# Seven products in a row, then thirty-six: the order of TensorE's work in the second half of a feed-forward part

## The chip, the core and the metric

One core of a Trainium2 chip runs the kernel. A core has TensorE (PE in the profile: matmuls; PEld are its weight loads), VectorE (DVE), ScalarE (ACT), GpSimd (POOL) and SyncE (SP, which here only issues transfers). Each works through its own list of instructions in order and waits on semaphores for the others. Matmuls write PSUM; VectorE and ScalarE read PSUM and SBUF, GpSimd works on SBUF alone. The metric is the time on the device in microseconds (us), as the median over runs.

## The reference

Attention with a decay, then a feed-forward part on its result. Of the first, what matters here is only that it delivers `x`, 4608 tokens of 512 values. The second is

```python
h = x @ w_in                                   # 512 -> 2048
sp = np.maximum(h, 0.0) + np.log1p(np.exp(-np.abs(h)))
g = h * erf(sp)
return (g @ w_out).astype(np.float32)          # 2048 -> 512
```

## The kernel before

**Tiling.** The 4608 tokens are six pairs of blocks of 384. Half of `w_in` and `w_out` (1024 of the 2048 middle columns) is in SBUF at a time, so that each pair is visited twice: visits 0 to 5 with the first half, 6 to 11 with the second. A visit has four units (`HU` = 4), one for each 256 middle columns; unit n belongs to visit v = n // 4 and has the place k = n % 4 in it. There are 48 units, 0 to 47. The change bears on units 25 to 47.

**Products with w_in.** All values are split into a high and a low part (float32r), and a product is taken as three matmuls, high by high, high by low, low by high. The 2x2 blocks of (256 columns) x (768 tokens) are computed with seven products instead of eight (a Strassen scheme, `PRODUCTS`, line 63). One product (line 186) is six matmuls of 128x384 into PSUM. Two PSUM tiles, m0 and m1, serve a unit, and each is started twice in it: products 0 and 2 go into one, 1 into the other, 3 and 5 into the second again, 4 and 6 into the first. In between, `consume` takes the partial result out: after product 0 ScalarE copies it to `sa` (line 199); after 1 VectorE adds `sa` to it and gets `sb` (202); after 2 ScalarE copies the first `h` (204); after 3 VectorE makes `sc` (207); after 4, 5 and 6 it makes the other three `h` (210). So product i + 2 may start only when the result after product i has been taken out.

**Activation.** For the four `h` tiles of the unit before, ScalarE computes softplus (214), then erf (217), with a table load ahead of each; VectorE multiplies by `h` (`gate`, 220); ScalarE writes the high half `gh` (229) and GpSimd the low half `gl` (230).

**Products with w_out.** `down(n - 2)` (line 249) is 36 matmuls of 128x512 from `gh` and `gl` of the unit before the last, into six PSUM tiles `y`, one for each 128 tokens (tb = 0 to 5), six matmuls for each. They are summed over the four units of a visit. After the visit's last unit, `finish` takes each `y` out: in the first six visits it stores it to a DRAM tile `part_d`; in the last six VectorE adds the stored part, which lies in a tile `yo` (line 279), and SP stores the sum (280). There are four `yo` buffers for six token blocks. `want_part` (260) loads the first four at the start of the unit k = 0 that follows; the loads for tb = 4 and 5 are issued by `finish` right behind the stores of tb = 0 and 1, into the buffers that these stores read, and so wait on SP until the store has landed.

**The next visit's x.** Four tiles `t` are loaded in the unit with k = 1; two sums (`x_sum`, 112 and 114) follow in k = 2, the splits into high (ScalarE, line 122, 128x768) and low parts (`rest_x`, 127, 128x768) and two more sums (131) in k = 3 and the next k = 0. The seven x tiles have one buffer each, so that a tile is overwritten as soon as the product of the unit k = 3 that reads it is done.

**Order.** Nothing is left to a scheduler (`manual_schedule`): each engine runs the instructions in the order in which the program lists them. `step` lists a unit: for each of seven places a product and its `consume`, side work, and a share of the 36 `down` matmuls by the table `YCUT`: six behind each product except the sixth, behind which there are none.

Of the kernel before, what the change touches and what calls it, by code (L numbers as in the profile page):

```python
# [56 lines left out]
NPAIR = NT // PAIR  # L57
NU = FF // (2 * P)
HU = NU // 2
# [10 lines left out]
SOFTPLUS = "softplus"  # L70
# [6 lines left out]
class Moe:  # L77
# [206 lines left out]
    def do(self, *at):  # L284
        for f in self.work.pop(at, []):
            f()

    def step(self, n):

        v, k = divmod(n, HU)  # L290
        up, gates = n < self.n, 1 <= n <= self.n
        downs = self.down(n - 2) if n >= 2 else iter(())
        after = v + 1 < len(self.visits) and n < self.n
        if n >= 2 and (n - 1) % HU == HU - 1 and self.visits[(n - 1) // HU][1]:
            v_ = (n - 1) // HU
            for tb in range(NTB if v_ == len(self.visits) - 1 else 4):
                self.want_part(v_, tb)
        if gates:
            self.softplus(n - 1, 0)
            self.softplus(n - 1, 1)  # L300
        if after and (n == 2 or v and k == 1):
            self.load_x(v + 1)
        for i in range(7):
            if up:
                self.product(n, i)
                self.consume(n, i)
            if up and v and k == 0 and i == 0:
                self.last_x(v, 0)
            if gates and i == 0:
                for q in (2, 3):  # L310
                    self.softplus(n - 1, q)
                for q in range(4):
                    self.erf(n - 1, q)
            if after and i < 2:
                self.next_x(v + 1, k, i)
            if gates and i in (1, 3):
                for q in (i - 1, i):
                    self.gate(n - 1, q)
            if up and v and k == 0 and i in (1, 2):
                self.last_x(v, i)  # L320
            if gates and i == 2:
                self.do(n, "abs")
            if up and i == (2 if gates else 5):
                self.nc.scalar.preload_act_table_set(SOFTPLUS)
            if gates and i in (2, 3):
                for q in (2 * i - 4, 2 * i - 3):
                    self.halve(n - 1, q)
            if after and i >= 2:
                self.next_x(v + 1, k, i)
            for _ in range(YCUT[i + 1] - YCUT[i]):  # L330
                next(downs, None)
            self.do(n, i)
            yield
        for _ in downs:
            pass
        if self.reload:
            self.reload(n)
# [648 lines left out]
```

## Time and profile before

| | |
|---|---|
| median of three runs | 1058.92 us (1057.91 to 1060.29) |
| the profiled execution | 1058.24 us, span of its instructions 1055.9 us |
| granted TensorE clock | 1.000 over the span |
| PE, PEld busy | 1046.7 us (99%), 933.9 us (88%) |
| DVE, ACT, POOL busy | 761.2 (72%), 778.0 (74%), 499.1 us (47%) |
| matmuls with w_in (L186) | 2016 |
| matmuls with w_out (L249) | 1152 with gh, 576 with gl |

The span runs from the first to the last instruction; the profiled execution's time has 2.3 us beside it. A row of the timeline has the start in us from the span's start, the duration of the merged run of equal instructions, the engine, the line, what is written and read, and how many instructions; in brackets, how long the engine had been idle and what ended that. Matmuls overlap, and the end of one is modelled, so the distance between starts tells what one costs. Unit n of 7 to 47 starts 15.64 us behind unit n - 1; unit 25 starts at 675.99 us and unit 47 at 1020.07 us.

### The profile page before, as it was taken

The page shows a single profiled execution, that of the slowest core. Times are in us where ns is not written, and L with a number is a line of the kernel's source. Part 1 is how long each engine was busy: PE and PEld are TensorE (multiplying, and loading weights), DVE is VectorE, ACT ScalarE, POOL GpSimd, SP SyncE. Part 2 cuts the span into 40 slices and gives each one's busy share as a digit, 9 for nine tenths or more (in the row PEclk, how much of TensorE's full clock was granted, in tenths as well). Part 3 has the DMA queues.
Part 4 walks back from the last instruction along what each step waited for, and adds up shares of the span by engine and source line. Part 5 has one row for each costly group of instructions (what it writes and reads, how often), then busy time and mean ns, then how long its engine had stood idle before and what let it go on. Part 6 is the DMA issues. An engine that isn't in the chain of part 4 may idle for free.

```text
span 1055.9 us, 23199 instructions
## 1 busy us (share of the span) xinstructions
PE 1046.7 (99%) x8554; PEld 933.9 (88%) x8554; DVE 761.2 (72%) x1767; ACT 778.0 (74%) x1668; POOL 499.1 (47%) x650
## 2 busy tenths in 40 slices
PE   9999999999999999999999999999999999999998
PEld 7889889888898888999988899899888899999987
DVE  6899999999867887776778755547565565756533
ACT  6988888898867778777778866767675675766662
POOL 3679899987544463453535333223223313313322
PEclk9999999999999999999999999999999999999999
DMA  7587978777513242523505164631303123130121
GB/s 270 198 287 258 325 254 280 243 241 241 189 67 131 71 168 71 210 100 120 180 28 213 60 226 163 229 121 60 120 16 115 51 67 113 61 120 1 50 91 60
DMA packets 70368, 154.91 MB, mean 147 GB/s; under 512 B 6960, under 2 KB 19504, under 8 KB 69232
## 3 DMA queue, kind: packets, MB, share of 16 engines
q1 hardware_dynamic: 70256, 153.43, 41.9%
q8 instruction: 68, 1.11, 0.4%
q14 instruction: 44, 0.36, 0.1%
HBM read 113.41 MB, written 39.99 MB: 145 GB/s over the span
## 4 chain that ended last, share of the span: by engine, by line
PE 90%; DVE 6%; ACT 2%; issue 1%; DMA 0%; POOL 0%; DVEq 0%; ACTq 0%; POOLq 0%
PE y L249 36%; PE m L186 31%; PE s L666 10%; PE o L774 8%; PE xy L737 3%; DVE pr L696 2%; PE s L673 2%; PE z L737 1%; DVE x L127 1%; DVE e L220 1%; ACT L217 0%; ACT e L217 0%; PE o L737 0%; DVE pt L746 0%; DVE ta L131 0%
## 5 line engine op out<-in xcount | busy, mean ns | idle before, releaser
L230 POOL TENSOR_TENSOR gl<-e,gh 128x384 fp32r<-128x384 f32 x192 | 223.1, 1192 | 392.4 <-ACT gh L229 392.4
L186 PE MATMUL m<-x,wi 128*128 128x384 f32 x2016 | 396.9, 335 | 1.0 <-DVE h L210 0.9
L186 PEld LDWEIGHTS m<-x,wi 128*128 128x128 f32 x2016 | 357.9, 188 | 28.0 <-DVE h L210 3.1
L249 PE MATMUL y<-wo,gh 128*128 128x512 f32 x1152 | 358.0, 392 | 0.0
L249 PEld LDWEIGHTS y<-wo,gh 128*128 128x128 f32 x1152 | 212.2, 188 | 27.9
L249 PE MATMUL y<-wo,gl 128*128 128x512 f32 x576 | 228.6, 397 | 0.0
L721 POOL TENSOR_SCALAR pr<-pr,st 128x576 f32<-128x576 f32 (+4 forms) x320 | 166.5, 542 | 62.7 <-DVE st L714 32.5
L708 ACT ACTIVATE pr<-pr,st 128x576 f32<-128x576 f32 (+3 forms) x320 | 175.5, 553 | 2.0 <-DVE st L696 2.0
L220 DVE TENSOR_TENSOR e<-e,h 128x384 f32<-128x384 f32 x192 | 142.5, 783 | 21.8 <-ACT e L217 21.8
L696 DVE CUSTOM_DVE_ANT_0 pr<-s,c 128x576 f32<-128x576 f32 (+3 forms) x320 | 136.8, 487 | 14.9 <-PE s L673 13.6
L229 ACT CAST gh<-e 128x384 fp32r<-128x384 f32 x192 | 92.0, 512 | 62.8 <-DVE e L220 61.8
L214 ACT ACTIVATE e<-h 128x384 f32<-128x384 f32 x192 | 94.0, 521 | 59.9 <-DVE h L210 55.6
L666 PE MATMUL s<-k,q 64*128 64x320 f32 (+4 forms) x768 | 128.5, 406 | 1.4 <-DVE st L696 0.7
L249 PEld LDWEIGHTS y<-wo,gl 128*128 128x128 f32 x576 | 107.9, 187 | 22.9
L666 PEld LDWEIGHTS s<-k,q 64*128 64x128 f32 x768 | 91.0, 186 | 27.0 <-issue 12.3
L202 DVE TENSOR_TENSOR sb<-m,sa 128x384 f32<-128x384 f32 x48 | 26.7, 557 | 106.4 <-PE m L186 88.9
L774 PE MATMUL o<-pt,v 128*64 128x128 f32 (+1 forms) x1920 | 102.5, 259 | 0.0
L774 PEld LDWEIGHTS o<-pt,v 128*64 128x64 f32 x1920 | 93.7, 137 | 4.5 <-issue 0.2
L127 DVE TENSOR_TENSOR x<-t,x 128x768 fp32r<-128x768 f32 x77 | 80.8, 1061 | 21.5 <-ACT x L122 21.5
L748 ACT COPY pt<-xy 128x1024 f32<-128x1024 f32 x64 | 64.8, 1012 | 36.9 <-PE xy L737 35.5
L210 DVE TENSOR_TENSOR h<-m,sb 128x384 f32<-128x384 f32 x96 | 53.0, 552 | 50.3 <-PE m L186 50.3
L217 ACT ACTIVATE e<-e 128x384 f32<-128x384 f32 x192 | 84.9, 513 | 0.5
(113 smaller groups left out, 1133.5 us busy)
## 6 DMA issues: line engine op xcount, KB each, us to landing
v<-in_vp_dram SPq DMA_DIRECT2D x32, 576.0 KB, 4.5
c<-cum_d SPq DMA_DIRECT2D x60, 288.0 KB, 5.8
t<-xt_d SPq DMA_DIRECT2D x44, 384.0 KB, 5.4
q<-in_q_dram SPq DMA_DIRECT2D x32, 320.0 KB, 4.9
k<-in_k_dram SPq DMA_DIRECT2D x32, 288.0 KB, 5.4
xt_d<-xo SPq DMA_DIRECT2D x32, 288.0 KB, 2.3
part_d<-yo SPq DMA_DIRECT2D x36, 256.0 KB, 3.1
yo<-part_d SPq DMA_DIRECT2D x34, 256.0 KB, 3.2
```

The lines of the kernel that those rows point to most:

```text
L127: eng.tensor_tensor(out=x[:, 1, kd], in0=self.src[r][:, kd], in1=x[:, 0, kd].bitcast(F32), op=ALU.subtract)
L186: nc.tensor.matmul(out=ps, lhsT=w[:, wp, ws], rhs=x[:, xp, kd], start=first and kd == 0 and j == 0, stop=kd == 1 and j == 2 and i in (1, 2 ...
L214: self.nc.scalar.activation(out=e, in_=self.h[n, q], func=AF.Softplus)
L220: self.nc.vector.tensor_mul(self.e[n, q], self.e[n, q], self.h.pop((n, q)))
L229: nc.scalar.copy(out=gh, in_=e)
L230: nc.gpsimd.tensor_tensor(out=gl, in0=e, in1=gh.bitcast(F32), op=ALU.subtract)
L249: yield nc.tensor.matmul(out=y[tb], lhsT=g[:, cs], rhs=w[:, f, wp], start=first, stop=last)
L666: nc.tensor.matmul(out=s[j][:, at:at + k1 - k0], lhsT=q[HALF[j], PAD + START[i]:PAD + END[i]], rhs=k[HALF[j], k0:k1], start=at in (0, 192, ...
L696: nc.vector.tensor_tensor_reduce(out=to[:, ::-1] if j else to, in0=score, in1=decay_, scale=-0.125, scalar=BIG, op0=ALU.add, op1=ALU.min, ...
L708: nc.scalar.activation(out=seg, in_=seg, func=AF.Exp, bias=st[:, 0, j, m:m + 1], scale=-1.0, accum_out=st[:, 1, j, m:m + 1])
L721: nc.gpsimd.tensor_scalar(out=seg, in0=seg, scalar1=st[:, 2, j, m:m + 1], scalar2=1.0, op0=ALU.mult, op1=ALU.mult)
L774: nc.tensor.matmul(out=o[h, to:to + 64 * (1 + (a < b))], lhsT=v[:, ch, h], rhs=src, start=m == 0, stop=m == len(parts) - 1, skip_group_che ...
```

## The change

Units 25 to 47 are listed by a new function, `long_step`. The seven products with their `consume` come back to back; the 36 `down` matmuls come behind the seventh. The side work has new places: all gates, halves and `finish` are listed behind the seventh product, and so are the sums and splits of x for k = 3 that need it; `rest_x` of x tiles 4 and 6 goes to GpSimd instead of VectorE. Which instructions there are, and on what data, does not change otherwise.

```diff
--- before.py
+++ after.py
@@ -285,8 +285,71 @@
         for f in self.work.pop(at, []):
             f()
 
+    def long_step(self, n):
+
+        v, k = divmod(n, HU)
+        dve, pool = self.nc.vector, self.nc.gpsimd
+        after = v + 1 < len(self.visits)
+        if (n - 1) % HU == HU - 1:
+            for tb in range(4):
+                self.want_part(v - 1, tb)
+        if after and k == 1:
+            self.load_x(v + 1)
+        for i in range(7):
+            self.product(n, i)
+            self.consume(n, i)
+            if k == 0 and i == 0:
+                self.split_x(v, 3)
+                self.rest_x(v, 2, dve)
+            elif k == 0 and i == 1:
+                self.rest_x(v, 3, dve)
+            elif after and k == 2 and i < 2:
+                self.x_sum(v + 1, i, dve)
+            elif after and k == 3 and i == 0:
+                self.split_x(v + 1, 0)
+            elif after and k == 3 and i == 1:
+                self.rest_x(v + 1, 0, dve)
+            elif after and k == 3 and i == 2:
+                self.split_x(v + 1, 1)
+            if i == 2 or i == 0 and k in (1, 2):
+                for q in range(4 if i == 2 else 2):
+                    if (n - 1, q) not in self.e:
+                        self.softplus(n - 1, q)
+        for q in range(4):
+            self.erf(n - 1, q)
+        self.nc.scalar.preload_act_table_set(SOFTPLUS)
+        x = after and k == 3
+        if x:
+            self.late_sum(v + 1, 0, dve)
+            self.rest_x(v + 1, 1, dve)
+            self.split_x(v + 1, 5)
+        for q in (0, 1):
+            self.gate(n - 1, q)
+        for q in (0, 1):
+            self.halve(n - 1, q)
+        if x:
+            self.rest_x(v + 1, 5, dve)
+            self.late_sum(v + 1, 1, dve)
+            self.split_x(v + 1, 4)
+        for q in (2, 3):
+            self.gate(n - 1, q)
+        for q in (2, 3):
+            self.halve(n - 1, q)
+        if x:
+            self.rest_x(v + 1, 4, pool)
+            self.split_x(v + 1, 6)
+            self.rest_x(v + 1, 6, pool)
+            self.split_x(v + 1, 2)
+        for _ in self.down(n - 2):
+            pass
+        self.reload(n)
+        yield
+
     def step(self, n):
 
+        if HU * NPAIR < n < self.n:
+            yield from self.long_step(n)
+            return
         v, k = divmod(n, HU)
         up, gates = n < self.n, 1 <= n <= self.n
         downs = self.down(n - 2) if n >= 2 else iter(())
```

Three places show what moved. The names carry the unit's or visit's number, then the tile's: `m33_1` is product 1 of unit 33, `y7_0` is block tb = 0 of visit 7, `gh31_2` is of unit 31.

**PE, the start of unit 33 (k = 1).** Before:

```order
L186 MATMUL m33_0_11119<-x8_0_10853,wi1_1_9512 128x384 x6
L249 MATMUL y7_0_10702<-wo1_3_10098,gh31_0_11030 128x512 x2
L249 MATMUL y7_0_10702<-wo1_3_10098,gl31_0_11031 128x512
L249 MATMUL y7_0_10702<-wo1_3_10098,gh31_1_11034 128x512 x2
L249 MATMUL y7_0_10702<-wo1_3_10098,gl31_1_11035 128x512
L186 MATMUL m33_1_11142<-x8_5_10907,wi1_1_9512 128x384 x6
L249 MATMUL y7_1_10703<-wo1_3_10098,gh31_0_11030 128x512 x2
L249 MATMUL y7_1_10703<-wo1_3_10098,gl31_0_11031 128x512
L249 MATMUL y7_1_10703<-wo1_3_10098,gh31_1_11034 128x512 x2
L249 MATMUL y7_1_10703<-wo1_3_10098,gl31_1_11035 128x512
L186 MATMUL m33_0_11119<-x8_1_10909,wi1_1_9512 128x384 x6
L249 MATMUL y7_2_10704<-wo1_3_10098,gh31_0_11030 128x512 x2
```

and now:

```order
L186 MATMUL m33_0_11115<-x8_0_10826,wi1_1_9512 128x384 x6
L186 MATMUL m33_1_11128<-x8_5_10897,wi1_1_9512 128x384 x6
L186 MATMUL m33_0_11115<-x8_1_10846,wi1_1_9512 128x384 x6
L186 MATMUL m33_3_11149<-x8_4_10911,wi1_1_9512 128x384 x6
L186 MATMUL m33_4_11158<-x8_6_10924,wi1_1_9512 128x384 x6
L186 MATMUL m33_3_11149<-x8_2_10927,wi1_1_9512 128x384 x6
L186 MATMUL m33_4_11158<-x8_3_10982,wi1_1_9512 128x384 x6
L249 MATMUL y7_0_10775<-wo1_3_10098,gh31_0_11052 128x512 x2
L249 MATMUL y7_0_10775<-wo1_3_10098,gl31_0_11053 128x512
L249 MATMUL y7_0_10775<-wo1_3_10098,gh31_1_11056 128x512 x2
L249 MATMUL y7_0_10775<-wo1_3_10098,gl31_1_11057 128x512
```

The six `y` matmuls that stood between two products stand behind all seven; product 2 (the second `m33_0`) follows product 0 with one product between them.

**DVE, the end of unit 33 and the start of unit 34 (k = 1 and 2).** Here L279 is `finish` of visit 7 and L112 and L114 are `x_sum` of visit 9. Before:

```order
L207 TENSOR_TENSOR sc33_11197<-m33_3_11190,sb33_11149 128x384
L220 TENSOR_TENSOR e32_2_11128<-e32_2_11128,h32_2_11098 128x384
L220 TENSOR_TENSOR e32_3_11130<-e32_3_11130,h32_3_11076 128x384
L279 TENSOR_TENSOR yo7_2_10966<-y7_2_10704,yo7_2_10966 128x512
L210 TENSOR_TENSOR h33_3_11224<-m33_4_11217,sc33_11197 128x384
L279 TENSOR_TENSOR yo7_3_10968<-y7_3_10705,yo7_3_10968 128x512
L210 TENSOR_TENSOR h33_1_11240<-m33_3_11190,sb33_11149 128x384
L210 TENSOR_TENSOR h33_2_11248<-m33_4_11217,sb33_11149 128x384
L279 TENSOR_TENSOR yo7_4_11155<-y7_4_10706,yo7_4_11155 128x512
L279 TENSOR_TENSOR yo7_5_11182<-y7_5_10707,yo7_5_11182 128x512
L112 TENSOR_TENSOR t9_4_11114<-t9_2_11112,t9_3_11113 128x768
L202 TENSOR_TENSOR sb34_11301<-m34_1_11294,sa34_11271 128x384
```

and now:

```order
L220 TENSOR_TENSOR e32_0_11124<-e32_0_11124,h32_0_11001 128x384
L220 TENSOR_TENSOR e32_1_11126<-e32_1_11126,h32_1_11035 128x384
L220 TENSOR_TENSOR e32_2_11145<-e32_2_11145,h32_2_11043 128x384
L220 TENSOR_TENSOR e32_3_11147<-e32_3_11147,h32_3_11027 128x384
L279 TENSOR_TENSOR yo7_0_10965<-y7_0_10775,yo7_0_10965 128x512
L279 TENSOR_TENSOR yo7_1_10967<-y7_1_10776,yo7_1_10967 128x512
L279 TENSOR_TENSOR yo7_2_10969<-y7_2_10777,yo7_2_10969 128x512
L279 TENSOR_TENSOR yo7_3_10971<-y7_3_10778,yo7_3_10971 128x512
L279 TENSOR_TENSOR yo7_4_11216<-y7_4_10779,yo7_4_11216 128x512
L279 TENSOR_TENSOR yo7_5_11226<-y7_5_10780,yo7_5_11226 128x512
L112 TENSOR_TENSOR t9_4_11110<-t9_2_11108,t9_3_11109 128x768
L202 TENSOR_TENSOR sb34_11281<-m34_1_11274,sa34_11267 128x384
```

The six L279 stood among the unit's L207 and L210; they now stand in one run behind the four gates (L220), right ahead of L112 and of unit 34's first `sb`. SP's list has the same order at this place before and now: store of `yo7_0`, load of `yo7_4`, store of `yo7_1`, load of `yo7_5`, then the other four stores.

**POOL, units 31 and 32 (k = 3 and 0).** Before:

```order
L230 TENSOR_TENSOR gl30_0_10873<-e30_0_10817,gh30_0_10872 128x384
L230 TENSOR_TENSOR gl30_1_10877<-e30_1_10819,gh30_1_10876 128x384
L230 TENSOR_TENSOR gl30_2_10900<-e30_2_10830,gh30_2_10899 128x384
L230 TENSOR_TENSOR gl30_3_10904<-e30_3_10832,gh30_3_10903 128x384
L230 TENSOR_TENSOR gl31_0_11031<-e31_0_10970,gh31_0_11030 128x384
```

and now:

```order
L230 TENSOR_TENSOR gl30_0_10902<-e30_0_10848,gh30_0_10901 128x384
L230 TENSOR_TENSOR gl30_1_10906<-e30_1_10850,gh30_1_10905 128x384
L230 TENSOR_TENSOR gl30_2_10916<-e30_2_10852,gh30_2_10915 128x384
L230 TENSOR_TENSOR gl30_3_10920<-e30_3_10854,gh30_3_10919 128x384
L127 TENSOR_TENSOR x8_4_10911<-t8_4_10530,x8_4_10911 128x768
L127 TENSOR_TENSOR x8_6_10924<-t8_2_10528,x8_6_10924 128x768
L230 TENSOR_TENSOR gl31_0_11053<-e31_0_11003,gh31_0_11052 128x384
```

The two L127, which VectorE ran before, stand behind the four `gl` of unit 30 and ahead of those of unit 31; products 3 and 4 of unit 32 read what they write.

## The prediction, on record before the changed kernel ran

> **What bounds the kernel now.** I read the page first, then the sums over units 25 to 47 alone, then TensorE's timeline.
>
> ```profile
> span 1055.9 us, 23199 instructions
> PE 1046.7 (99%) x8554; PEld 933.9 (88%) x8554; DVE 761.2 (72%) x1767; ACT 778.0 (74%) x1668; POOL 499.1 (47%) x650
> 675.99:1035.70 359.71, 359.71 (x1795) 323.32 (x1794) 204.07 (x294) 233.80 (x409) 104.05 (x92) 1.00 0.24 81
> ```
>
> The third row is the stage that the change touches: 359.71 us, PE busy in all of it (the second number), the clock at 1.00. Nothing is waited for there, so TensorE's own pace sets the end, and a gain can only come from that pace. A busy PE is not yet PE at its peak, so I look at the distances between starts. First from product 5 of unit 23 to that of unit 24, then the last 36 matmuls of the kernel, which run without products between them:
>
> ```profile
> 656.87 2.25 PE L186 MATMUL m<-x,wi 128*128 128x384 f32 x12
> 658.96 0.63 PE L249 MATMUL y<-wo,gh 128*128 128x512 f32 x2
> 660.35 1.21 PE L186 MATMUL m<-x,wi 128*128 128x384 f32 x6
> 661.39 0.63 PE L249 MATMUL y<-wo,gh 128*128 128x512 f32 x2
> 662.78 1.20 PE L186 MATMUL m<-x,wi 128*128 128x384 f32 x6
> 672.51 2.25 PE L186 MATMUL m<-x,wi 128*128 128x384 f32 x12
> ...
> 1037.08 0.62 PE L249 MATMUL y<-wo,gh 128*128 128x512 f32 x2
> 1050.68 0.62 PE L249 MATMUL y<-wo,gh 128*128 128x512 f32 x2
> ```
>
> One product takes 661.39 - 660.35 = 1.04, two in a row 658.96 - 656.87 = 2.09: no gain there. A block of six `y` takes 662.78 - 661.39 = 1.39. In the tail 60 `y` lie between the two rows: 13.60 us, 1.36 for six. So each change from products to `y` costs 0.03. A unit is 672.51 - 656.87 = 15.64 now.
>
> **The change, part by part.** *TensorE's pace.* Five of six changes go in each unit. A unit is then 7 x 1.04 + 6 x 1.36 + 0.03 = 15.47, less by 0.17; over 23 units **-3.8 us**. This is all that there is to gain.
>
> *The hand-over of PSUM.* Product i + 2 starts 2.08 behind product i and needs its result taken out.
>
> ```profile
> 1032.40 2.07 PE L186 MATMUL m<-x,wi 128*128 128x384 f32 x11
> 1034.51 0.56 DVE L210 TENSOR_TENSOR h<-m,sb 128x384 f32<-128x384 f32 x1 [0.48 <-PE m L186]
> ...
> 332.10 0.54 DVE L210 TENSOR_TENSOR h<-m,sb 128x384 f32<-128x384 f32 x1
> 332.70 1.31 PE L186 MATMUL m<-x,wi 128*128 128x384 f32 x6 [0.16 <-DVE h L210]
> 333.84 0.63 PE L249 MATMUL y<-wo,gh 128*128 128x512 f32 x2
> ```
>
> A product ends 1.21 behind its start (its row above); VectorE starts 0.04 later (1034.47 to 1034.51), takes 0.56, and a waiting matmul starts 0.06 behind that (332.64 to 332.70): 1.87 of 2.08. The cover that is gone, 1.39 of `y`, is not needed as long as the engine is free within 0.21 us. Cost 0; if every one of the five hand-overs missed by 0.1, it would be 23 x 5 x 0.1 = 11.5. The last two rows also price a restart: that product takes 1.14 instead of 1.04, so 0.1 for each stall.
>
> *The stores and loads behind `finish` (k = 1, felt in k = 2).* Times from here on are from the first product of the unit k = 1. VectorE takes the last `h` out at 7.5 to 8.0, then come four gates, then six L279.
>
> ```profile
> 743.04 1.03 DVE L220 TENSOR_TENSOR e<-e,h 128x384 f32<-128x384 f32 x2 [0.21 <-ACT e L217]
> 743.99 1.28 DVE L279 TENSOR_TENSOR yo<-y,yo 128x512 f32<-128x512 f32 x2
> 744.70 0.35 SPq L280 DMA_DIRECT2D out_dram<-yo  x1
> 746.70 0.33 SPq L260 DMA_DIRECT2D yo<-part_d  x1
> 747.12 0.38 SPq L280 DMA_DIRECT2D out_dram<-yo  x1
> 750.11 0.32 SPq L260 DMA_DIRECT2D yo<-part_d  x1
> ...
> 807.26 0.35 SPq L280 DMA_DIRECT2D out_dram<-yo  x1
> 813.72 0.32 SPq L260 DMA_DIRECT2D yo<-part_d  x1
> ...
> yo<-part_d SPq DMA_DIRECT2D x34, 256.0 KB, 3.2
> ```
>
> Unit 29 began at 738.55 (675.99 + 4 x 15.64), so its first L279 stood at 5.4 and its first store was issued at 6.15; SP holds the load for tb = 4 until that store has landed (2.00), holds the next store behind that load, and the load for tb = 5 until that store has landed: 5.41 from the first store's issue to the last load's, 6.46 in unit 33; then 3.2 to landing (page, part 6). Now the first L279 comes behind the four gates: some 0.5 apart by the row of two, from 8.0, 8.5 and 9.0; the fourth, at 9.5, finds GpSimd's first `gl` begun at 9.4 and waits for it (below), to 10.8. Store at 11.55, last load issued at 17.0, landed at 20.2. The sixth L279 waits for it, and behind it on VectorE stand `x_sum` and unit 34's `sb`, without which product 3 cannot start:
>
> ```profile
> L279 DVE TENSOR_TENSOR yo<-y,yo 128x512 f32<-128x512 f32 x30 | 20.0, 681 | 1.2 <-PE y L249 1.2
> L112 DVE TENSOR_TENSOR t<-t,t 128x768 f32<-128x768 f32 x5 | 4.7, 949 | 0.0
> ```
>
> 20.2 + 0.64 + 0.88 (both a little under their duration, as the next overlaps) + 0.56 + 0.06 = 22.35; product 3 was due at 15.47 + 3.12 = 18.59. Stall 3.75 us in units 30, 34, 38 and 42; in 46 there is no `x_sum`, 2.9. Sum **+17.9**. Low end: gates without the collision (0.8 earlier) and a landing shorter than its median by 0.4 (an estimate), 2.55 each, 11.8 in all; high end: 6.46 in the chain, 4.8 each, 23 in all. I take the middle, since unit 29's row is the shorter of the two and the landing is a median.
>
> *GpSimd's two rests (k = 3, felt in k = 0).* GpSimd and VectorE get in each other's way on SBUF operands:
>
> ```profile
> 778.46 4.58 POOL L230 TENSOR_TENSOR gl<-e,gh 128x384 fp32r<-128x384 f32 x4 [11.20 <-ACT gh L229]
> 778.84 2.34 DVE L220 TENSOR_TENSOR e<-e,h 128x384 f32<-128x384 f32 x2
> 782.50 1.36 DVE L127 TENSOR_TENSOR x<-t,x 128x768 fp32r<-128x768 f32 x1 [0.85 <-ACT x L122]
> L444 POOL TENSOR_TENSOR llo<-ltop,lhi 128x512 fp32r<-128x512 f32 x8 | 10.4, 1299 | 45.7 <-PE m L186 30.3 <-ACT lhi L443 15.4
> L127 POOL TENSOR_TENSOR x<-ta,x 128x384 fp32r<-128x384 f32 x6 | 6.0, 1001 | 0.0
> ```
>
> Two gates took 2.34 beside `gl` against 1.03 above, and four `gl` 4.58 against 4 x 1.0: they run in turns. An L127 that began under a `gl` took 1.36 instead of 0.95. The Trainium skill (SBUF — State Buffer, "SBUF: two separate sides") states that the port pair which the two share is locked for a whole instruction, and the other blocks. By that rule a long instruction on GpSimd holds VectorE off for all of it, and the sum is the one below; were the port given up in between, it would be the low end. The trace agrees for 384 columns (1.36); for 768 on GpSimd no run here shows it yet.
>
> From 384 and 512 columns (1.00 and 1.30) 768 come to about 1.85. ScalarE's list sets the beginning:
>
> ```profile
> 740.16 0.94 ACT L214 ACTIVATE e<-h 128x384 f32<-128x384 f32 x2
> 741.12 1.28 ACT L217 ACT_TABLE_LOAD   x1
> 742.41 1.77 ACT L217 ACTIVATE e<-e 128x384 f32<-128x384 f32 x4
> L122 ACT CAST x<-t 128x768 fp32r<-128x768 f32 x35 | 27.5, 828 | 0.0
> ```
>
> In k = 3: `h` out at 3.3 to 3.8, split of x1 to 4.4, four softplus to 6.1, table to 7.4, erfs to 9.1, table to 10.4, split of x5 to 11.1, `gh` 0 and `gl` 0 from 11.7. On VectorE stand now rest x5, a sum, gates 2 and 3, each in turns with `gl` 0 and 1: gate 3 ends at 15.6, `gl` 2 starts at 15.8, `gl` 3 ends at 17.8. The rest of x4 goes in turn with VectorE's rest of x2 and ends at 20.3, that of x6 with the rest of x3 and ends at 22.9. ScalarE, held by the late `gh`, copies unit k = 0's `sa` at 17.5 to 18.0, 0.8 late, which moves product 2 by 0.5. Product 3 (reads x4) could start at 18.59 + 0.5 and waits until 20.4, 1.2; product 4 (reads x6) then waits from 21.4 to 22.9, 1.4. Stall 3.1 in units 28, 32, 36, 40 and 44: **+15.6**. Low end: no turns, all ends by 19.7, 0.1 each; high end: 2.0 for the rest on GpSimd, 3.45, 17.3 in all. The rows are nearest to the high end, since VectorE's work beside GpSimd's is the same kind.
>
> *Restarts:* 5 x 3 + 5 = 20 stalls at 0.1, **+2.0**. Everything else (other places of gates and halves, `want_part`, `load_x`) has over a unit until it is read: 0.
>
> **Sum:** -3.8 + 17.9 + 15.6 + 2.0 = +31.7 us on the profiled execution's 1058.24, 1089.9. The median of the runs is 0.7 above that execution, so **1090 us**.
>
> **The rivals.**
> - *Only the loads stall, GpSimd is in time* (the low end of that part): 1058.9 - 3.8 + 17.9 + 0.5 = 1073.5. For it: `gl` alone takes 1.0; against it: the 4.58 and 2.34 above. Chance 0.17.
> - *Faster:* if the sixth L279 starts by 18.59 - 0.06 - 0.56 - 0.88 - 0.64 = 16.45, unit 34's `sb` is in time, and if GpSimd also is, what remains is 1058.9 - 3.8 = 1055.1. What decides is whether the last load lands by 16.45; the chain of 5.41 + 3.2 would have to start at 7.8, when the first `y` is not yet summed (7.28 + 1.39). Chance 0.05.
> - *The hand-overs miss* by 0.1 each, beside the stalls: 1090 + 11.5 = 1101.5. For it: only 0.21 of slack; against it: the steps are the same in every row that I looked at. Chance 0.06.
> - *The clock falls behind the long stalls:* if TensorE ran at half speed for the four products behind each stall in k = 2, that is 5 x 4 x 1.04 = 21 more, 1111. Nothing in the trace bears it out; the one idle time over 1 us had no drop of the clock near it:
>
> ```profile
> PE idle L806 <- POOL ident masks.py:199: 1.4, 1, 1.4
> ```
>
> The Trainium skill (TensorE: Matmul & The Clock Gate, "What's actually happening") puts the fall to half at an idle window of about 3.4 us, and 3.75 lies just above it. No run here shows it. Chance 0.07.
>
> **How the numbers follow.** The forecast has 0.65, with its own range 1079 to 1099 from the two terms' ends. Below 1069 lie the faster case and the lower part of the first rival, above 1101 the clock and part of the hand-overs: together 2 in 10. Range 1069 to 1101. About 0.2% is what a measurement can tell from no change; faster by more 0.04, within it 0.02, slower 0.94.
>
> **What would show it.** In the changed profile: `y` rows 0.68 apart for three in all units; units k = 1 and k = 3 at 15.47; PE idle in k = 2 ahead of product 3, ended by VectorE's `sb`, with the sixth L279 idle until a transfer; PE idle in k = 0 ahead of products 3 and 4, ended by GpSimd's L127. It is wrong if units k = 2 or k = 0 take under 16 us, if products without a stall are over 1.05 apart, or if the clock leaves 1.00.

## The result, and the profile after

The changed kernel takes 1090.23 us (median of 6 runs, 1085.29 to 1096.44), the kernel before beside it 1059.51 us (6 runs, 1057.91 to 1060.57). The ratio is 1.0291 with a 95% interval of 1.0255 to 1.0327: slower by 2.9%. The forecast of 1090 is met as a time; its terms are not all met, and misses cancel.

The first lines of the changed kernel's page:

```profile
span 1083.5 us, 23179 instructions
PE 1051.8 (97%) x8554; PEld 936.0 (86%) x8554; DVE 747.2 (69%) x1757; ACT 775.7 (72%) x1668; POOL 521.9 (48%) x660
```

The sum over units 25 to 47 (from and to, us, then busy us and instructions of PE, PEld, DVE, ACT and POOL, granted clock, share of the DMA engines, GB/s):

```profile
675.12:1063.30 388.18, 365.62 (x1795) 325.92 (x1794) 189.61 (x284) 233.26 (x412) 127.27 (x102) 0.99 0.22 75
```

The stage grew from 359.71 to 388.18 us, by 28.5. PE, which was busy in all of it before, is idle for 22.6 us of it (388.18 - 365.62), and the granted clock is no longer 1.00. TensorE's waits in that stage name who ends the idle time (us in total, how often, the longest):

```profile
PE m L186 <- DVE sb L202: 10.0, 5, 2.4
PE m L186 <- POOL x L127: 9.8, 10, 1.2
PE m L186 <- ACT sa L199: 2.8, 5, 0.6
```

That is 20 stalls, where the prediction counted 20: one in each of the five units k = 2 (ahead of product 3, ended by VectorE's `sb`), three in each of the five units k = 0 (the wait ahead of product 2 ended by ScalarE, those ahead of products 3 and 4 by GpSimd). From the distances between the first products of neighbouring units, against 15.64 before:

| units | length now, us | sum against before |
|---|---|---|
| the 12 without a stall, base of all 23 | 15.51 (25 and 26: 15.48 and 15.54) | 23 x -0.13 = -3.0 |
| k = 0: 28, 32, 36, 40, 44 | 18.89, 18.91, 18.88, 18.91, 18.89 | 16.9 over the base |
| k = 2: 30, 34, 38, 42, 46 | 19.82, 17.83, 17.65, 19.75, 17.07 | 14.6 over the base |

The three come to +28.5. Outside the stage the two profiled executions differ by 1.4 the other way, so that this one is 1085.29 - 1058.24 = 27.1 slower; it is the fastest of the six.

**Units k = 0.** The timelines of GpSimd, VectorE and TensorE around the start of unit 32 (791.37; the last row of an engine counts only up to the end of the stretch shown, so that it can be short):

```profile
787.80 3.06 POOL L230 TENSOR_TENSOR gl<-e,gh 128x384 fp32r<-128x384 f32 x2 [13.88 <-ACT gh L229]
791.91 1.98 POOL L230 TENSOR_TENSOR gl<-e,gh 128x384 fp32r<-128x384 f32 x2 [1.04 <-ACT gh L229]
793.85 5.09 POOL L127 TENSOR_TENSOR x<-t,x 128x768 fp32r<-128x768 f32 x2
...
795.14 2.12 DVE L127 TENSOR_TENSOR x<-t,x 128x768 fp32r<-128x768 f32 x1
...
791.37 2.27 PE L186 MATMUL m<-x,wi 128*128 128x384 f32 x12
794.20 1.52 PE L186 MATMUL m<-x,wi 128*128 128x384 f32 x7 [0.55 <-ACT sa L199]
796.50 1.31 PE L186 MATMUL m<-x,wi 128*128 128x384 f32 x6 [0.78 <-POOL x L127]
799.00 2.20 PE L186 MATMUL m<-x,wi 128*128 128x384 f32 x11 [1.18 <-POOL x L127]
```

In unit 31 (which began at 791.37 - 15.51 = 775.86) the first `gl` begins at 11.94, the last ends at 18.0, and the two rests end at 20.6 and 23.1; the prediction had 11.7, 17.8, 20.3 and 22.9. Beside each other the 768-wide subtracts take turns: 5.09 for the two on GpSimd, and 2.12 for one on VectorE that takes 0.95 alone.

**Units k = 2.** SP, GpSimd, VectorE and TensorE around unit 34 (first product at 825.79; unit 33 began at 810.28):

```profile
820.84 0.35 SPq L280 DMA_DIRECT2D out_dram<-yo  x1
822.85 0.33 SPq L260 DMA_DIRECT2D yo<-part_d  x1
823.27 0.38 SPq L280 DMA_DIRECT2D out_dram<-yo  x1
826.22 0.32 SPq L260 DMA_DIRECT2D yo<-part_d  x1
...
819.92 4.09 POOL L230 TENSOR_TENSOR gl<-e,gh 128x384 fp32r<-128x384 f32 x4 [11.59 <-ACT gh L229]
...
818.26 1.95 DVE L220 TENSOR_TENSOR e<-e,h 128x384 f32<-128x384 f32 x4
820.13 1.28 DVE L279 TENSOR_TENSOR yo<-y,yo 128x512 f32<-128x512 f32 x2
829.07 0.69 DVE L279 TENSOR_TENSOR yo<-y,yo 128x512 f32<-128x512 f32 x1 [2.70 <-DMA yo<-part_d]
829.68 0.95 DVE L112 TENSOR_TENSOR t<-t,t 128x768 f32<-128x768 f32 x1
830.55 0.55 DVE L202 TENSOR_TENSOR sb<-m,sa 128x384 f32<-128x384 f32 x1
...
825.79 3.31 PE L186 MATMUL m<-x,wi 128*128 128x384 f32 x18
831.15 1.14 PE L186 MATMUL m<-x,wi 128*128 128x384 f32 x5 [2.05 <-DVE sb L202]
```

Here is the whole chain: a store, a load behind it, a store, a load, the sixth L279 that waited 2.70 for that load, `x_sum`, `sb`, product 3. It is the chain that the prediction named, but it starts earlier than there: the four gates run in 1.95 without a break, and GpSimd's first `gl` begins at 819.92, behind the start of the fourth gate (818.26 + 3 x 0.47 = 819.67).

**The clock.** Units 30 and 42 are 2 us longer than 34 and 38, with idle times that are nearly the same (2.45 and 2.40 against 2.05 and 1.84). The stage in pieces of 3.41 us shows why (same columns as above; the seventh is the granted clock):

```profile
758.69:762.10 3.41, 0.96 (x6) 0.64 (x5) 2.37 (x4) 2.67 (x5) 0.00 (x0) 1.00 0.94 341
762.10:765.51 3.41, 3.41 (x12) 3.41 (x12) 1.07 (x2) 2.97 (x5) 0.00 (x0) 0.51 0.84 296
...
895.20:898.60 3.40, 1.62 (x10) 1.30 (x8) 2.01 (x4) 2.61 (x7) 0.00 (x0) 1.00 0.91 337
898.60:902.00 3.40, 3.33 (x19) 3.33 (x20) 1.99 (x4) 3.37 (x6) 0.00 (x0) 1.00 0.93 316
```

Behind unit 30's stop TensorE has half its clock for one piece (12 matmuls where 19 fit); behind unit 38's it has not.

### The profile page after: what moved, and what is told of

Same layout as the page of the kernel before. It is cut to its first block, busy times and chain, and to the rows that moved or that the text cites. A ratio compares the mean times of both kernels' runs of the same rounds, so it can differ in the third digit from the quotient of the medians.

```text
span 1083.5 us, 23179 instructions
## 1 busy us (share of the span) xinstructions
PE 1051.8 (97%) x8554; PEld 936.0 (86%) x8554; DVE 747.2 (69%) x1757; ACT 775.7 (72%) x1668; POOL 521.9 (48%) x660
## 4 chain that ended last, share of the span: by engine, by line
PE 69%; issue 9%; DVE 8%; POOL 5%; ACT 5%; DMA 3%; SPq 0%; DVEq 0%; POOLq 0%; ACTq 0%
PE y L249 24%; PE m L186 21%; PE s L729 9%; PE o L837 8%; DMA out_dram<-yo 3%; POOL gl L230 3%; PE xy L800 3%; POOL x L127 2%; DVE pr L759 2%; PE s L736 2%; ACT e L217 1%; DVE e L220 1%; PE z L800 1%; ACT L217 1%; ACT e L214 1%
## 5 line engine op out<-in xcount | busy, mean ns | idle before, releaser
L186 PE MATMUL m<-x,wi 128*128 128x384 f32 x2016 | 387.4, 339 | 23.6 <-DVE sb L202 10.0
L220 DVE TENSOR_TENSOR e<-e,h 128x384 f32<-128x384 f32 x192 | 127.8, 714 | 18.4 <-ACT e L217 18.4
L199 ACT COPY sa<-m 128x384 f32<-128x384 f32 x48 | 23.0, 479 | 131.2 <-PE m L186 131.0
L214 ACT ACTIVATE e<-h 128x384 f32<-128x384 f32 x192 | 90.9, 521 | 23.6 <-DVE h L210 18.0
L127 DVE TENSOR_TENSOR x<-t,x 128x768 fp32r<-128x768 f32 x67 | 75.6, 1136 | 26.9 <-ACT x L122 26.9
```

The costliest lines, as they stand in the source:

```text
L127: eng.tensor_tensor(out=x[:, 1, kd], in0=self.src[r][:, kd], in1=x[:, 0, kd].bitcast(F32), op=ALU.subtract)
L186: nc.tensor.matmul(out=ps, lhsT=w[:, wp, ws], rhs=x[:, xp, kd], start=first and kd == 0 and j == 0, stop=kd == 1 and j == 2 and i in (1, 2 ...
L214: self.nc.scalar.activation(out=e, in_=self.h[n, q], func=AF.Softplus)
L220: self.nc.vector.tensor_mul(self.e[n, q], self.e[n, q], self.h.pop((n, q)))
```

## The experiments

The theory after the result: the loss has two independent causes, the chain of stores and loads in k = 2 and GpSimd's rests in k = 0, and on top of the first a fall of the clock behind some of the stops. The rivals: that back-to-back products themselves pay (hand-overs of PSUM, TensorE's pace), that only one of the two causes is real, and that the clock does not fall because of the stop. All edits are against the changed kernel, and each run stands beside runs of the kernel before on its chip.

| run | median, us (lowest to highest) | ratio to before (95%) |
|---|---|---|
| rests on VectorE | 1086.69 (1083.65 to 1089.33) | 1.0258 (1.0230 to 1.0285) |
| own buffers | 1072.24 (1071.96 to 1073.19) | 1.0125 (1.0103 to 1.0147) |
| both | 1067.10 (1066.30 to 1067.84) | 1.0074 (1.0055 to 1.0093) |
| TensorE kept busy | 1084.98 (1083.74 to 1086.23) | 1.0243 (1.0222 to 1.0263) |
| x first, with own buffers | 1056.07 (1054.00 to 1060.00) | 0.9975 (0.9960 to 0.9990) |
| the same, `sc` twice | 1068.25 (1065.85 to 1069.25) | 1.0085 (1.0064 to 1.0107) |
| the change again | 1090.98 (1086.65 to 1093.11) | 1.0295 (1.0270 to 1.0320) |
| both, `gl` later | 1058.24 (1056.62 to 1060.39) | 1.0002 (0.9992 to 1.0011) |

### The two rests back on VectorE

```diff
-            self.rest_x(v + 1, 4, pool)
+            self.rest_x(v + 1, 4, dve)
             self.split_x(v + 1, 6)
-            self.rest_x(v + 1, 6, pool)
+            self.rest_x(v + 1, 6, dve)
```

> The two rests of x4 and x6 go back to VectorE at the place where the change lists them; all else is the changed kernel. Theory (GpSimd, taking turns with VectorE, ends them too late for products 3 and 4 of the unit k = 0): these units go from 18.9 us to about 17.6, since VectorE's queue and the late copy sa still hold product 2 and 3 for 0.7 and 1.4; 5 x 1.3 = 6.5 less, 1084 as a median. Units k = 2 stay at 17.1 to 19.8. Rival (ScalarE is too full in k = 3, and its late copies alone cause the stall): units k = 0 stay at 18.9, 1090.

TensorE's waits in the stage:

```profile
PE m L186 <- DVE sb L202: 16.9, 10, 3.5
PE m L186 <- ACT sa L199: 2.8, 5, 0.6
```

GpSimd ends no wait any more. Units k = 0 take 17.65 instead of 18.9, or 19.22 where the clock fell. The choice of engine is thus 1.25 of the 3.4 us; the other 2.14 stay, now ended by VectorE's `sb` (1.0 of idle time) and ScalarE's `sa` (0.55): the rests still stand behind four `gl` that take turns with VectorE's work. The units k = 2 were longer here, 18.13 to 20.88 (17.24 in unit 46), although nothing was changed for them: the clock fell in three of them instead of two, and the chain was longer in some. So the median fell by some 4 us instead of the 6.5 expected, and the intervals of the two ratios overlap; the length of the units k = 0 is what shows the gain. In unit 34, the longest, SP's rows of the same chain were:

```profile
820.99 0.35 SPq L280 DMA_DIRECT2D out_dram<-yo  x1
823.96 0.33 SPq L260 DMA_DIRECT2D yo<-part_d  x1
824.39 0.38 SPq L280 DMA_DIRECT2D out_dram<-yo  x1
827.62 0.32 SPq L260 DMA_DIRECT2D yo<-part_d  x1
```

It took 6.63 from the first store's issue to the last load's, where the changed kernel's took 5.38: each load could be issued 2.97 and 3.23 behind the store ahead of it, instead of 2.01 and 2.95. The same chain can cost over 1 us more in another execution.

### All six parts of `y` loaded ahead, with buffers of their own

```diff
         if (n - 1) % HU == HU - 1:
-            for tb in range(4):
+            for tb in range(NTB):
                 self.want_part(v - 1, tb)
...
+        elif tb >= 4:
+            yo = self.eb.tile([P, DM], F32, name=f"yo{v}_{tb}", tag="top", bufs=3)
...
-        if tb + 4 < NTB and v + 1 < len(self.visits):
-            self.want_part(v, tb + 4)
```

> In the second half of the visits the stored parts for tb = 4 and 5 get buffers of their own (those of the weight work, which is over by then), and all six are loaded at the start of the unit k = 0; finish issues stores only. Theory (the sixth addition waits for a load that waits for a store, and the next unit's sb stands behind it): units k = 2 go from 17.1 to 19.8 us to 15.5, the clock stays at 1.000 there, units k = 0 stay at 18.9; 1090 - 11 for the stalls - 6 for the clock = 1073. Rival (products in a row outrun the engines that empty PSUM, wherever the side work stands): units k = 2 stay over 16.5, above 1080.

TensorE's waits in the stage:

```profile
PE m L186 <- POOL x L127: 9.8, 10, 1.2
PE m L186 <- ACT sa L199: 2.8, 5, 0.6
```

Two of its units, 30 and 32, whole:

```profile
755.90:771.40 15.50, 15.50 (x79) 14.06 (x78) 7.08 (x12) 8.72 (x16) 4.07 (x4) 1.00 0.39 137
786.91:807.35 20.44, 17.93 (x79) 15.52 (x78) 8.77 (x12) 11.94 (x21) 11.46 (x8) 0.92 0.21 77
```

Every unit k = 2 is now 15.51, and PE is busy throughout (15.50 of 15.50). Taking the store out of the load's way takes 1090.98 - 1072.24 = 18.7 us off (across two chips) with no instruction removed. So the chain of stores and loads was the whole cause there, the clock's falls in these units included. One fall is left, in unit 32, which has the three shorter stops of k = 0 and no long one.

### Both

```diff
-            self.rest_x(v + 1, 4, pool)
+            self.rest_x(v + 1, 4, dve)
...
-            self.want_part(v, tb + 4)
```

> Both of the edits before: the rests of x4 and x6 on VectorE, and own buffers for tb = 4 and 5. Theory: units k = 1, 2, 3 at 15.5, k = 0 at 17.6; 1059.5 - 23 x 0.13 + 5 x 2.1 = 1067. Rival (products in a row outrun the engines that empty PSUM): all units are longer than 15.64 where a consume has company on its engine, and the sum stays over 1075.

TensorE's waits in the stage:

```profile
PE m L186 <- DVE sb L202: 5.0, 5, 1.0
PE m L186 <- ACT sa L199: 2.8, 5, 0.6
```

The units k = 0 take 17.65 (one 19.19 with a fall of the clock), all others 15.51. The two causes add: from the change's 1.0291 the single edits take 0.0033 and 0.0166, together 0.0199, and both at once take 0.0217; the intervals are some 0.002 to 0.004 wide on either side.

### TensorE kept busy in the stop of k = 2

Ten matmuls more, into the first `y` tile of the visit, whose own first matmul comes later in the unit and overwrites them; they stand ahead of product 3 in units 30, 34, 38, 42 and 46. No result changes.

```diff
+            if k == 2 and i == 3 and v > NPAIR:
+                self.keep_busy(v, k)
             self.product(n, i)
...
+        for _ in range(10):
+            self.nc.tensor.matmul(out=y[:, :TB], lhsT=self.wi[1, k][:, 0, 0, :P], rhs=self.x[v, 0][:, 0, 0],
+                                  start=True, stop=True, skip_group_check=True)
```

> The changed kernel with ten more matmuls of 128x384 (1.74 us) in the units 30, 34, 38, 42 and 46, ahead of product 3, where TensorE stands still for 2 us or more; they go into a y tile whose real first matmul starts afresh, so the result is the same. Theory (the clock falls because TensorE stood still for too long): the extra matmuls lie in the stall and cost nothing, the idle time left is under 1 us, the clock stays at 1.000, and the median falls from 1090 to 1081 to 1085, with a smaller spread, though work was added. Rival (the clock and the spread have another cause): the clock still falls in some runs and the median stays at 1090. Second rival (the stall is not there in all runs): the matmuls add up to 5 x 1.74 = 8.7, 1099.

The end of the stop of unit 30 on TensorE's timeline:

```profile
762.09 1.90 PE L293 MATMUL y<-x,wi 128*128 128x384 f32 x10
764.65 1.69 PE L186 MATMUL m<-x,wi 128*128 128x384 f32 x8 [0.67 <-DVE sb L202]
```

Units 30 and 28 whole:

```profile
758.94:777.10 18.16, 17.49 (x89) 15.77 (x88) 8.51 (x13) 8.93 (x16) 4.41 (x4) 1.00 0.37 132
723.10:743.40 20.30, 17.79 (x79) 15.38 (x78) 8.79 (x12) 11.96 (x21) 11.47 (x8) 0.92 0.22 78
```

Product 3 starts when it would have started anyway, but none of the five units k = 2 shows a fall: 18.21, 18.18, 18.27, 18.28 and 17.24. 50 matmuls more make the kernel about 5 us faster (1084.98 against 1090.23 and 1090.98, on other chips; the interval of the ratio lies wholly below that of the change run again and overlaps the lower end of the first one's). So the stop itself costs 18.2 - 15.5 = 2.7 us a unit in this execution, 1.7 in unit 46; what such units take beyond that with a fall was the clock. The one fall left is in a unit k = 0, to which nothing was added.

### The work on x first

All that products of the next unit k = 0 read is listed ahead of gates 2 and 3 in k = 3, on VectorE, and the `gh` and `gl` of the four gates go behind product 0 of the next unit. Own buffers as above.

```diff
+            if k == 0 and v > NPAIR and i == 0:
+                for q in range(4):
+                    self.halve(n - 2, q)
...
+            for q in (0, 1):
+                self.gate(n - 1, q)
+            self.rest_x(v + 1, 5, dve)
+            self.late_sum(v + 1, 1, dve)
+            for r in (4, 6, 2, 3):
+                self.split_x(v + 1, r)
+                self.rest_x(v + 1, r, dve)
+            for q in (2, 3):
+                self.gate(n - 1, q)
```

> The change with both causes taken away: own buffers for tb = 4 and 5 as in the experiment before, and in the unit k = 3 the work on the next x comes first: all splits on ScalarE and all rests on VectorE, gates 0 and 1 in the hole where VectorE waits for the split of x5, gates 2 and 3 last; the four halves (gh and gl) of that unit's gates move behind product 0 of the next unit, so that GpSimd's gl do not start while VectorE works on SBUF tiles. Theory (the stalls come from these two places alone, and the order of products is good by itself): every unit from 25 to 46 at 15.51, TensorE idle nowhere, clock 1.000; 1059 - 23 x 0.13 = 1056, so 0.3% faster than the kernel before. Rival (the order of products costs more than it brings, whatever stands beside it): units over 15.64, and the median over 1059.

The stage as a whole:

```profile
676.68:1033.30 356.62, 356.62 (x1795) 323.41 (x1794) 177.05 (x294) 232.82 (x412) 92.27 (x92) 1.00 0.23 82
```

A unit of it on TensorE's timeline:

```profile
785.24 7.47 PE L186 MATMUL m<-x,wi 128*128 128x384 f32 x42
792.55 0.63 PE L249 MATMUL y<-wo,gh 128*128 128x512 f32 x2
```

PE is busy in all of the stage and the clock is at 1.00: every unit takes 15.51, and 23 of them 356.62 against 359.71 before. Seven products back to back with every hand-over of PSUM in time: 7.31 us for 42 matmuls. This version is faster than both kernels: against the one before by 2.6 us in the median (ratio 0.9975, 0.9960 to 0.9990), of which the stage's 3.1 us, the pace, is the source.

### One addition twice

To measure the slack of the hand-over, VectorE's `sc` is computed twice in units 25 to 47 of the kernel above.

```diff
-            nc.vector.tensor_tensor(out=self.u4, in0=ps, in1=self.u2, op=ALU.add)
+            for _ in range(2 if HU * NPAIR < n < self.n else 1):
+                nc.vector.tensor_tensor(out=self.u4, in0=ps, in1=self.u2, op=ALU.add)
```

> The experiment just before, with the addition that makes sc done twice in units 25 to 47 (same operands, same result), to price the hand-over of PSUM: product 5 waits for it. By the prediction's rows it has 0.21 us to spare (1.87 of 2.08), and the second addition takes 0.48: product 5 is late by 0.27 and restarts for 0.1, so units go from 15.51 to 15.8 to 15.9, and the time by 6 to 9 us to 1062 to 1065. Rival (there is more to spare, as TensorE works ahead): units stay at 15.51, 1056.

TensorE's only wait in the stage:

```profile
PE m L186 <- DVE sc L208: 4.6, 23, 0.2
```

VectorE and TensorE in one unit, from the timeline:

```profile
777.16 1.15 DVE L208 TENSOR_TENSOR sc<-m,sb 128x384 f32<-128x384 f32 x2 [0.60 <-PE m L186]
775.75 2.42 PE L186 MATMUL m<-x,wi 128*128 128x384 f32 x13
778.37 1.83 PE L186 MATMUL m<-x,wi 128*128 128x384 f32 x9 [0.20 <-DVE sc L208]
```

The second addition adds 1.15 - 0.56 = 0.59, more than the 0.47 by which two gates in a row differ from one. Product 5's first matmul stands 13 behind the row's first; it comes 2.62 later (778.37 - 775.75) instead of 13 x 0.174 = 2.26, so 0.36 late. The hand-over therefore takes 2.08 + 0.36 - 0.59 = 1.85 without the doubling, a slack of 0.23; the prediction worked out 1.87 and 0.21. The units are 16.01, 0.50 longer: 0.36 and a restart of 0.14. Both are above what was expected (0.27 and 0.1), and so is the time, 1068.25 against 1062 to 1065: the second addition takes 0.59, where 0.48 had been assumed.

### The change again

No edit; the changed kernel on the chip of the two runs above.

> The changed kernel as it is, once more, beside the others on one chip, for the clock: units k = 2 where TensorE stood still for over 2.3 us have the clock halved for 3.4 us behind it, those with less do not; k = 0 at 18.9 where the clock stays, some 1.5 longer where it falls. Median 1085 to 1092, mean clock of the runs 0.989 to 1.000, and the longer runs are those with the lower clock. Rival (the spread is the transfers', not the clock's): no order between the clock and the time.

Units k = 2 of this execution: 19.88 (30), 19.95 (34), 19.68 (38), 18.18 (42), 17.17 (46); k = 0: 20.31, 20.47 and 20.44, then 18.88 and 18.91. Six units have a fall of the clock, where the first execution had two. Pieces of 3.41 us in units 28 and 42:

```profile
726.06:729.47 3.41, 1.79 (x9) 1.18 (x7) 2.58 (x2) 3.08 (x6) 3.41 (x2) 1.00 0.00 0
729.47:732.88 3.41, 3.07 (x10) 3.07 (x11) 0.56 (x1) 3.38 (x6) 0.29 (x1) 0.50 0.50 150
...
971.82:975.23 3.41, 1.83 (x11) 1.51 (x9) 1.26 (x2) 2.62 (x7) 0.00 (x0) 1.00 0.95 302
975.23:978.64 3.41, 2.59 (x15) 2.60 (x16) 2.38 (x5) 3.38 (x6) 0.00 (x0) 1.00 0.78 210
```

Unit 42 has the same stop as unit 38 (2.40 us idle against 2.33) and no fall: its stop lies across two pieces, for which the rows show 11 and 15 matmuls. Unit 28, whose three stops are 0.55, 0.78 and 1.18, has one. The expectation that the length of one stop decides falls with this; the counts at the end show what goes with a fall instead, how little ran within a piece. The median, 1090.98, lies in the expected range. The longer runs have the lower clock only by and large: 1093.11 at 0.991, 1092.15 at 0.995, 1090.98 at 0.993, 1087.62 at 1.000, 1086.65 at 0.998.

### The rests on VectorE, own buffers, and `gl` later

As "both", with the halves of unit k = 3 listed behind product 0 of the next unit, which leaves the order of x as the change has it.

```diff
-        for q in (0, 1):
+        for q in () if x else (0, 1):
             self.halve(n - 1, q)
...
+                if v > NPAIR:
+                    for q in range(4):
+                        self.halve(n - 2, q)
```

> The kernel with both edits (rests on VectorE, own buffers) and one more: the four halves of the unit k = 3 move behind product 0 of the next unit; the order of the work on x stays. It asks what still holds units k = 0 at 17.65. Theory (GpSimd's gl take turns with VectorE's work on SBUF tiles in k = 3, which makes gates 2 and 3 late, then gh on ScalarE, then sa and sb): the chain is gone, units k = 0 go to about 15.9 (what is left is the copy of the first h, late by 0.4 behind the moved gh), 1067 - 5 x 1.75 = 1058. Rival (VectorE's list in k = 3 is too long by itself, with two more rests): units k = 0 stay at 17.6, 1067.

TensorE's waits in the stage:

```profile
PE m L186 <- ACT h L204: 0.9, 5, 0.2
```

That is the only wait left, and the median is as expected. Against "both", 17.65 of k = 0 become 16.0 by this edit alone. Gates 2 and 3 in unit 31 of "both" (beside `gl`) and of this run:

```profile
784.49 1.83 DVE L220 TENSOR_TENSOR e<-e,h 128x384 f32<-128x384 f32 x2
...
781.83 1.02 DVE L220 TENSOR_TENSOR e<-e,h 128x384 f32<-128x384 f32 x2
```

From the unit's first product they start at 14.06 and 13.22 and end 1.65 apart, as the sum ahead of them took turns with `gl` too (1.78 against 0.95). So the 2.14 which stayed when the rests went back to VectorE go with the four halves' place for the most part, and the rows show GpSimd's `gl` in turns with VectorE's work. The edit takes `gh` off ScalarE's list in k = 3 as well; what that alone brings was not measured apart.

## Why the prediction was right, and where it was wrong

| term | predicted | measured in the profiled execution |
|---|---|---|
| pace of 23 units | -3.8 | -3.0 |
| hand-overs of PSUM | 0 | 0 |
| k = 0, with its restarts | 15.6 + 1.5 | 16.9 |
| k = 2, with its restarts, at full clock | 17.9 + 0.5 | about 11.4 |
| falls of the clock | 0 | about 3.1 |
| sum | 31.7 | 28.4 |

The falls of the clock are two here, taken out of units 30 and 42 at 1.6 each, an estimate by the price that k = 0 shows in the repeated run (20.31, 20.47 and 20.44 against 18.89: 1.4 to 1.6).

**The pace** was right in kind. The one change from products to `y` that is left costs 0.07 rather than 0.03: with it a unit is 15.51, where 42 products and 36 `y` at 7.28 and 8.16 make 15.44. Before, six changes cost 15.64 - 15.44 = 0.20, so the five saved are worth 0.13 a unit.

**The hand-overs** cost nothing, and the slack was right to 0.02, by the run with `sc` twice. This rival (1101.5) is excluded: x first runs all seven back to back with PE never idle.

**k = 0** was right step by step. Products 2, 3 and 4 were put 0.5, 1.2 and 1.4 late; by the starts in unit 32 they are 0.74, 1.09 and 1.45 late (the rows at 796.50 and 799.00 begin with the second matmul of products 3 and 4), 3.28 in all, and the unit is 3.40 longer. The choice of the end near the high one, by the rows in which the two engines take turns, held: a rest on GpSimd took 2.5 in turns, where 1.85 had been worked out for one alone, and all ends lie within 0.3 of those worked out. What the prediction did not say is how the 3.4 splits: the first run above puts 1.25 down to the engine of the rests, the last puts 1.65 down to the halves (`gh` and `gl`) ahead of them. The Trainium skill (SBUF — State Buffer, "SBUF: two separate sides") has it that whichever of the two engines comes first holds the shared port pair for its whole instruction; the rows now agree for 768 columns too, 2.12 against 0.95 on VectorE. The rival "only the loads stall" is excluded by own buffers, where nothing but k = 0 is left and costs 18.9 a unit.

**k = 2** is the step that failed. The mechanism held at each link: removing the store ahead of the load removes every stall of these units. Its size did not. The step is the passage "the fourth, at 9.5, finds GpSimd's first `gl` begun at 9.4 and waits for it (below), to 10.8". GpSimd's first `gl` began at 819.92 - 810.28 = 9.64, behind the fourth gate's start at 9.38, and the four gates ran in 1.95 without a break; the first L279 stood at 820.13 - 810.28 = 9.85. This was no accident of one unit: in all 20 units k = 1 behind unit 28 of the four profiled executions that have this chain, `gl` begins at 9.64 and the fourth gate at 9.38. ScalarE's list, from which the 9.4 for `gl` came, ran some 0.25 later than worked out. The chain of 5.41 was right here (5.38) and the landing shorter than its median (829.07 - 826.22 = 2.85 instead of 3.2). Product 3 came at 20.87 instead of 22.35: 1.0 of the 1.5 is the collision that did not occur, 0.35 the landing, the rest the steps behind. So the low end that the prediction gave, 2.55 each, was near (2.1 to 2.7). A collision that the working decided by 0.1 us should have been counted as open, not as met. The spread of the chain was real as well: 5.38 here, 6.63 in one unit of the run with the rests on VectorE.

**The clock** had a chance of 0.07 and a price of 21. It came, so that the prediction's own last sign of being wrong, a clock that leaves 1.00, is there. It came in another form: not four products behind every stall, but one stretch of 3.41 us at half the clock behind some of them, 1.4 to 1.6 us each, twice in the first profiled execution and six times in the repeated one (two runs whose mean clock is shown as 1.000 had none), and in k = 0 too, where the prediction had not looked for it. The condition that it cited from the Trainium skill (TensorE: Matmul & The Clock Gate, "What's actually happening"), an idle window of about 3.4 us, was not needed: a stop of 2.45 was enough, in a stretch for which the row shows 6 matmuls. The same section of the Trainium skill states that the window runs free of the program. The traces agree: the two falls of the first execution, 762.15 and 966.95, lie 60 x 3.413 us apart, and from unit 25's start the raster stands 1.7 us in there and 2.6 in the repeated execution.

So k = 2 was put some 7 too high, the clock 3 too low in the profiled execution (some 9 in the repeated one), and the pace 0.8 too high a gain. For the profiled execution itself the forecast, 1089.9, was 4.6 too high; it is met by the median only because that lies 4.9 above this execution, where 0.7 had been put. That the time came out to 0.3 is luck. How much of the 4.9 is the clock and how much the chain's spread stays open: runs whose mean clock is shown as 1.000 took 1086.44 and 1087.62, those at 0.989 to 0.991 took 1091.98 to 1096.44. An estimate: a fall takes half of 3.41 us from the mean clock of some 1090, 0.0016, and costs about 1.5 us; with the falls so counted taken out, the eleven runs of the changed kernel lie at 1082 to 1088, so that both have a share. In the sums of the prediction some roundings are loose (23 x 0.17 is 3.9, 5 x 3.1 is 15.5, 1089.9 + 0.7 is 1090.6); none moves the forecast by more than 0.6.

## What to carry to other kernels

An order that packs one engine's work must be followed through the lists of all the others: here the pace was worth 3 us and a load behind a store on one queue, and x behind work that nobody needed yet, cost 31, some 3 of it through the clock; with those two put right the same packing gains 2.6 in the median. Where two events that the working puts within 0.1 us of each other decide a term, give both outcomes their weight. A stop of TensorE of 2 to 3 us cost more than itself here when most of it fell into one stretch of the clock's raster; ten matmuls of no use to the result, put into the gap, took that part away.

## What the runs showed of the hardware that was not expected

- **The clock's raster.** (A row of the view by pieces counts a matmul in both pieces that it reaches into; here each counts once, where it begins.) In the profiled executions of the changed kernel, of its repeat, of both single edits, of both together and of the one kept busy, 15 stretches at half the clock lie in units 25 to 47, each 3.41 us long and on a raster of 3.413 us. Counting the matmuls that began in the stretch ahead (about 20 products or 15 `y` fit; stretches that are themselves at half the clock are left out): with up to 7 all 10 were followed by a fall, with 8 four of 5, with 9 one of 9, with 10 or more none of 629. A stop of 2.40 us across two stretches had no fall behind it, so that the cost of a stop depends on where it lies in the raster.
- **The stop need not be in one piece.** Three stops of 0.55, 0.78 and 1.18 us in one unit were followed by a fall in three of these executions (in one, three or one of five units), and by none in the first.
- **A second addition in a row that writes the same tile** took 0.59 with 0.56 for one alone, where the second of two gates on other tiles takes 0.47 (1.02 for two, 0.55 for one), and one L279 behind another, which read PSUM as `sc` does, 0.59 with 0.69 for one alone. That the common tile is the reason was not tested.
- **GpSimd and VectorE in turns at 768 columns:** 2.55 on GpSimd (5.09 for two) and 2.12 on VectorE, so that the subtract that VectorE began while GpSimd's ran took more than twice its 0.95.
